# Layer 1's last chunks in another order of tiles, and layer 2's block products in rows of 14

## The chip, the cores and the metric

The kernel runs on one core of a Trainium2 chip. The metric is the device time of one execution in microseconds (us). Three runs of the kernel before gave 894.57, 895.60 and 896.61 us.

The engines are named as the profile names them: PE is TensorE (PEld its weight loads), DVE is VectorE, ACT is ScalarE, POOL is GpSimd and SP is SyncE, which here does nothing but issue transfers. Each engine takes its instructions in program order; PE, DVE, ACT and POOL run beside each other and wait for each other through semaphores.

## The reference

Windowed attention feeds a two-layer feed-forward pair. The attention comes first (4 batches, 8 heads, 576 positions, a window of 128); its output, 2304 tokens of 512 numbers, goes through two layers of the same form with different activations:

```python
def _moe_ref(x, w_in, w_out):
    h = x @ w_in                       # 2304x512 by 512x2048
    g = np.maximum(0.01 * h, h)
    return g @ w_out                   # 2304x2048 by 2048x512

def _moe2_ref(x, w_in, w_out):
    h = x @ w_in
    g = h * (1.0 / (1.0 + np.exp(-1.702 * h)))
    return g @ w_out
```

## The kernel before

The whole kernel is one hand-written order: `tick` advances a step counter, and `after(d, fn)` puts an instruction `d` steps later in the streams. Whatever is emitted earlier stands earlier in the queue of its engine. Every matrix operand is kept as a pair, a rounded part and a remainder (`hi` and `lo`), so each product is three passes (hi by hi, hi by lo, lo by hi).

**Layer 1.** The tokens lie in five tiles, t0 to t4, of 384, 512, 512, 512 and 384 columns; the 2048 hidden features lie in eight chunks of 256. `rounds` lists the pairs (chunk, tile). A round is two groups of `mm1` (L517, 12 matmuls each) and, one round later, four groups of `mm2` (L541, 6 matmuls each), whose result is added into `y` by DVE (L551). Chunk weights sit in two pairs of tiles, wA and wB, so the weights of chunk c+2 go where those of chunk c were; `conv_w` builds them on ACT, DVE and POOL from 64-bit words.

**Layer 2.** The 2304 tokens form six blocks of 384, taken as three pairs. `unit_ops(i, p)` multiplies pair p by the input weights of chunk i with seven block products (a Strassen-like scheme), each one `product` call of 6 matmuls with 384 columns (L623). Five of the seven accumulate into the same PSUM bank, `X` (tag S), one goes to `Y` (tag O), two into `Q` (tag pt). Between them ACT copies `X` aside (`snap`, L644, into `sn`), DVE adds `Y` or `Q` to a copy (`finish`, L649), ACT applies the activation (`gate`, L635, into `u`), and `split` makes hi (ACT, L532) and lo (POOL, L143) of the result, `g` or `gm`. Four gates make the hidden values of one pair. They are the stationary operand of the six output groups `out2` of that pair (L691, 6 matmuls with 512 columns), two PSUM banks of tag mm; DVE (ACT for chunk 0) adds each group into `y` (L703, L701).

Units run as (chunk 0, pair 0), (0, 1), (1, 0), (1, 1) and so on to chunk 7, then pair 2 with chunks 0 to 7. In the 13 places of a unit the seven products stand at 0, 2, 3, 5, 7, 9 and 11; the other six places, `None` in the list, hold the six output groups of the unit before (in the first unit, the last six `mm2` groups of layer 1). The products use the tokens through 14 derived blocks: `build_x(p, pace)` makes seven of them for a pair with seven ACT conversions (L588, 128x768) and eleven DVE operations (L143, 128x768, `x<-y` and `y<-y`), spread over 11 times `pace` steps. Pair 0's blocks are begun ten groups before the first product, pair 1's seven steps after it. Block weights are reloaded from DRAM by SP after their last use (`load_in`, L609); the output weights of chunks 1 to 7 are built during layer 2 (`conv_out`) from `raw` words that `load_w` fetches.

Of the kernel before, what the change touches and what calls it, by code (L numbers as in the profile page):

```python
# [22 lines left out]
CB = 2  # L23
# [10 lines left out]
def attention_mlp_kernel(  # L34
# [144 lines left out]
    def conv_w(n, p):  # L179
# [6 lines left out]
        else:  # L186
            af, ops = to_f32(n, p, 4)
        hi, lo = wt[n][:, 2 * p], wt[n][:, 2 * p + 1]
        run(ops + [
            (10 if early else 7, lambda: nc.scalar.activation(hi, af, AF.Copy)),  # L190
# [442 lines left out]
    def gate(h, key):  # L633
        u = sb([128, 512], F32, "u", 2)[:, 0:TT]
        nc.scalar.activation(u, h, AF.Gelu_apprx_sigmoid)  # L635
        after(1, lambda: split(u, key, True))

    def unit_ops(i, p):
# [84 lines left out]
    rounds += [(0, c, t) for c in range(2, NCH) for t in range(NTT)]  # L723
# [13 lines left out]

    last1 = {c: j for j, (_, c, _) in enumerate(rounds)}
# [19 lines left out]
    def layer1():  # L758
# [4 lines left out]
        while pos2[0] < NR - 4 or q1 or q2 or todo or pending[0]:  # L763
# [24 lines left out]
    def layer2():  # L788
# [17 lines left out]
        units = [(c, p) for c in range(NCH) for p in range(2)] + [  # L806
            (NCH + c, 2) for c in range(NCH)]
        prev = [run_group] * len(groups)
        for k, (i, p) in enumerate(units):
            more = i + 1 < NCH  # L810
            for t, fn in enumerate(unit_ops(i, p)):
                if more and (p, t) in ((0, 6), (1, 4)):
                    load_w(NF + CB * (i + 1) + p, 1)
                if more and (p, t) == (1, 1):
                    conv_out(NF + CB * (i + 1))
                if 0 < i < NCH and (p, t) == (0, 1):
                    conv_out(NF + CB * i + 1)
# [164 lines left out]
```

## Time and profile before

| | us |
|---|---|
| runs (median of 3) | 895.60 |
| profiled execution, its own time | 896.78 |
| its span, first to last instruction | 894.8 |
| PE busy | 869.0 |
| DVE busy | 592.0 |
| ACT busy | 422.5 |
| POOL busy | 400.1 |

The 2 us between the profiled execution and its span lie outside all instructions. A row of a timeline gives the start in us from the span's start, the duration, the engine, the line with its operation, out<-in, the shape and the number of merged instructions; in brackets stands how long the engine sat idle before it and what released it. Matmuls overlap, so the pace of PE is read from the start of one group to the start of the next, not from their durations.

### The profile page before, as it was taken

The page shows a single profiled execution, that of the slowest core. Times are in us where ns is not written, and L with a number is a line of the kernel's source. Part 1 is how long each engine was busy: PE and PEld are TensorE (multiplying, and loading weights), DVE is VectorE, ACT ScalarE, POOL GpSimd, SP SyncE. Part 2 cuts the span into 40 slices and gives each one's busy share as a digit, 9 for nine tenths or more (in the row PEclk, how much of TensorE's full clock was granted, in tenths as well). Part 3 has the DMA queues.
Part 4 walks back from the last instruction along what each step waited for, and adds up shares of the span by engine and source line. Part 5 has one row for each costly group of instructions (what it writes and reads, how often), then busy time and mean ns, then how long its engine had stood idle before and what let it go on. Part 6 is the DMA issues. An engine that isn't in the chain of part 4 may idle for free.

```text
span 894.8 us, 15722 instructions
## 1 busy us (share of the span) xinstructions
PE 869.0 (97%) x5722; PEld 762.4 (85%) x5722; DVE 592.0 (66%) x1213; ACT 422.5 (47%) x1025; POOL 400.1 (45%) x441
## 2 busy tenths in 40 slices
PE   7789999999999999999999989999999999999997
PEld 4678888899898988888898878888898889889896
DVE  5889765368799998898943773555555557423433
ACT  4888885454334433543333466343434435442331
POOL 5787544345466757575542133333333233232221
PEclk6899999999999999999999999999999999999999
DMA  9764330242243353524250133453354345956562
GB/s 218 172 168 118 99 92 5 92 132 80 71 140 146 115 174 132 177 82 172 100 188 1 48 104 96 153 153 95 107 153 132 93 129 153 293 174 204 164 188 71
DMA packets 85533, 116.05 MB, mean 130 GB/s; under 512 B 40912, under 2 KB 51152, under 8 KB 84432
## 3 DMA queue, kind: packets, MB, share of 16 engines
q1 hardware_dynamic: 82064, 113.83, 42.2%
q10 hardware_dynamic: 3392, 1.21, 0.5%
q8 instruction: 46, 0.75, 0.3%
q14 instruction: 31, 0.25, 0.1%
HBM read 87.23 MB, written 27.79 MB: 129 GB/s over the span
## 4 chain that ended last, share of the span: by engine, by line
PE 82%; DVE 6%; POOL 3%; DMA 3%; issue 2%; ACT 2%; SPq 0%; POOLq 0%; DVEq 0%; ACTq 0%
PE mm L691 22%; PE S L623 11%; PE mm L541 10%; PE O L541 8%; PE pt L517 8%; PE S L517 8%; PE pt L623 5%; PE O L623 3%; PE mm L517 2%; PE O L477 2%; PE pt L442 2%; PE S L393 2%; POOL ca L175 1%; DMA y<-v 1%; DVE x L143 1%
## 5 line engine op out<-in xcount | busy, mean ns | idle before, releaser
L143 POOL TENSOR_TENSOR g<-u,g 128x384 fp32r<-128x384 f32 (+1 forms) x128 | 155.6, 1221 | 244.0 <-ACT g L532 168.3
L703 DVE TENSOR_TENSOR y<-y,mm 128x512 f32<-128x512 f32 x126 | 86.5, 686 | 119.0 <-PE mm L691 118.8
L691 PE MATMUL mm<-wB,g 128*128 128x512 f32 x432 | 118.8, 397 | 0.6 <-POOL g L143 0.6
L691 PE MATMUL mm<-wB,gm 128*128 128x512 f32 x432 | 116.7, 393 | 0.0
L175 POOL TENSOR_TENSOR ca<-ca,cb 128x512 f32<-128x512 f32 x59 | 81.8, 1387 | 69.0 <-DVE cb L173 64.1
L143 POOL TENSOR_TENSOR gm<-u,gm 128x384 fp32r<-128x384 f32 x48 | 48.7, 1024 | 128.9 <-ACT gm L532 80.1
L691 PEld LDWEIGHTS mm<-wB,g 128*128 128x128 f32 x432 | 80.8, 189 | 13.6 <-POOL g L143 1.0
L691 PEld LDWEIGHTS mm<-wB,gm 128*128 128x128 f32 x432 | 80.1, 188 | 12.9
L635 ACT ACTIVATE u<-sn 128x384 f32<-128x384 f32 x72 | 37.8, 525 | 97.0 <-DVE sn L649 61.2
L623 PE MATMUL S<-x,wA 128*128 128x384 f32 x384 | 78.0, 337 | 2.3 <-ACT x L588 1.8
L623 PEld LDWEIGHTS S<-x,wA 128*128 128x128 f32 x384 | 68.3, 188 | 6.8 <-ACT x L588 2.1
L532 ACT ACTIVATE g<-u 128x384 fp32r<-128x384 f32 (+1 forms) x128 | 70.6, 560 | 2.5 <-PE O L541 0.6
L551 DVE TENSOR_TENSOR y<-y,mm 128x512 f32<-128x512 f32 (+1 forms) x74 | 46.2, 624 | 37.1 <-PE mm L541 37.0
L541 PE MATMUL mm<-g,wA 128*128 128x512 f32 (+1 forms) x264 | 62.9, 372 | 3.3 <-POOL g L143 2.5
L541 PE MATMUL mm<-g,wB 128*128 128x512 f32 (+1 forms) x264 | 62.3, 371 | 0.0
L523 ACT ACTIVATE u<-S 128x512 f32<-128x512 f32 (+1 forms) x34 | 18.8, 553 | 85.6 <-PE S L517 85.6
L623 PE MATMUL pt<-x,wA 128*128 128x384 f32 x288 | 57.9, 335 | 0.0
L644 ACT ACTIVATE sn<-S 128x384 f32<-128x384 f32 x72 | 34.9, 485 | 46.4 <-PE S L623 44.5
L541 PEld LDWEIGHTS mm<-g,wA 128*128 128x128 f32 x264 | 47.6, 188 | 10.2 <-POOL g L143 3.2
L165 DVE TENSOR_SCALAR ca<-ca 128x512 f32<-128x512 f32 x62 | 30.5, 492 | 38.8 <-ACT ca L164 38.7
L623 PEld LDWEIGHTS pt<-x,wA 128*128 128x128 f32 x288 | 51.6, 188 | 4.4
L436 POOL TENSOR_SCALAR st<-st,sm 128x192 f32<-128x192 f32 (+2 forms) x100 | 43.3, 453 | 25.6 <-PE pt L442 8.0
(127 smaller groups left out, 1797.2 us busy)
## 6 DMA issues: line engine op xcount, KB each, us to landing
wA<-w7d SPq DMA_DIRECT2D x112, 256.0 KB, 3.1
w7d<-c SPq DMA_DIRECT2D x8, 1792.0 KB, 7.1
wB<-wod SPq DMA_DIRECT2D x36, 256.0 KB, 5.1
raw<-w1i SPq DMA_DIRECT2D x16, 512.0 KB, 3.5
raw<-w1o SPq DMA_DIRECT2D x16, 512.0 KB, 3.6
raw<-w2o SPq DMA_DIRECT2D x16, 512.0 KB, 4.5
raw<-w2i SPq DMA_DIRECT2D x16, 512.0 KB, 3.5
wod<-wB SPq DMA_DIRECT2D x28, 256.0 KB, 3.5
```

Of the source, the lines that this page charges most:

```text
L143: e.tensor_tensor(out=out, in0=in0, in1=in1, op=ALU.subtract)
L175: lambda: nc.gpsimd.tensor_tensor(out=af, in0=af, in1=bf, op=ALU.add),
L436: nc.gpsimd.tensor_scalar(w, w, sm[s][:, 3, m:m + 1], 1.0, op0=ALU.mult, op1=ALU.mult)
L517: nc.tensor.matmul(out=h, lhsT=w[:, a, k * 128:(k + 1) * 128], rhs=xt[t][:, b2, k], start=(m == 0), stop=(m == len(ops) - 1),)
L532: nc.scalar.activation(g[:, 0], u, AF.Copy)
L541: nc.tensor.matmul(out=y, lhsT=wt[c * CB + f][:, 2 + a, e * 128:(e + 1) * 128], rhs=gt[r, f][:, b2, :], start=(m == 0), stop=(m == len(ops ...
L551: nc.vector.tensor_tensor(out=acc, in0=acc, in1=y, op=ALU.add)
L623: nc.tensor.matmul(out=out, lhsT=w[:, 256 * a + 128 * k:256 * a + 128 * k + 128], rhs=x[:, b2, k], start=(start and m == 0), stop=(stop an ...
L635: nc.scalar.activation(u, h, AF.Gelu_apprx_sigmoid)
L644: nc.scalar.activation(st[name], st["X"], AF.Copy)
L691: nc.tensor.matmul(out=y, lhsT=gt[i, p, f, t][:, b2, e * 128:(e + 1) * 128], rhs=out_slot(i, f, a), start=(m == 0), stop=(m == len(ops) - 1),)
L703: nc.vector.tensor_tensor(out=acc, in0=acc, in1=yv, op=ALU.add)
```

## The change

There are two parts. In layer 1, `rounds` takes the last two chunks in another order: chunks 6 and 7 with tiles 0 and 1, then chunks 6 and 7 with tiles 2, 3 and 4. `layer2` then begins its own code when chunk 7 is through with tile 1 (the loop of `layer1` ends there), and pair 0's blocks are built from that point at a pace of 2 steps, 28 groups before the first product; the first weight loads wait until chunk 6 is through with all tiles. In layer 2, the chunks 1 to 6 no longer alternate: the fourteen products of pairs 0 and 1 run in a row, then the twelve output groups of both pairs. Chunk 7 and the units of pair 2 keep one unit at a time, with products and output groups in runs of up to four and of two. Beside this the activation is written over the copy `sn` in three gates of four, in place of a tile of its own, and pair 1's blocks lie in another order in memory.

```diff
-            (10 if early else 7, lambda: nc.scalar.activation(hi, af, AF.Copy)),
+            (10 if early else 7, split_hi),
...
+        xb[1] = [xb[1][n] for n in (0, 1, 4, 3, 5, 2, 6)]
...
-    def gate(h, key):
-        u = sb([128, 512], F32, "u", 2)[:, 0:TT]
+    def gate(h, key, u=None):
+        u = sb([128, 512], F32, "u", 2)[:, 0:TT] if u is None else u
...
-                after(1, lambda: gate(h, (i, p) + key))
+                after(1, lambda: gate(h, (i, p) + key, h))
...
-    rounds += [(0, c, t) for c in range(2, NCH) for t in range(NTT)]
+    rounds += [(0, c, t) for c in range(2, NCH - 2) for t in range(NTT)]
+    rounds += [(0, c, t) for ts in ((0, 1), (2, 3, 4)) for c in (NCH - 2, NCH - 1) for t in ts]
...
-        while pos2[0] < NR - 4 or q1 or q2 or todo or pending[0]:
+        while pos2[0] < first or q1 or q2 or todo or pending[0]:
...
+        build_x(0, 2)
+        loaded = False
         while len(groups) > 6:
             run_group()
             tick()
-            if begun is None and pos2[0] >= NR - 4:
-                begun = step[0]
-                build_x(0, 1.6)
-        assert begun is not None
-        after(max(1, begun + 16 - step[0]), lambda: build_x(1, 1.3))
+            if not loaded and pos2[0] >= last1[NCH - 2]:
+                loaded = True
+                for n in USE:
+                    load_in(0, n)
+        assert loaded
+        after(len(groups) - 4 + 5, lambda: build_x(1, 1.3))
...
+        for i in range(1, NCH - 1):
+            n0 = NF + CB * (i + 1)
+            lead = [None] * (len(prev) if i == 1 else 0)
+            w = [unit_ops(i, p) for p in range(2)]
+            ops = lead + [w[p][n] for p, n in (
+                (0, 0), (1, 0), (0, 5), (0, 4), (1, 4), (1, 5), (0, 3), (1, 3), (0, 1), (0, 6),
+                (1, 6), (1, 1), (0, 2), (1, 2))]
+            tail = [fn for t in (1, 0) for p in range(2) for fn in outs(i, p, t)]
+            last = i == NCH - 2
+            m = len(ops)
+            at = {m - 10: [raw_out(n0)], m - 6: [raw_out(n0 + 1)], m: [make_out(n0)],
+                  m + 5: [make_out(n0 + 1)]}
...
+            play(ops + (tail[:6] if last else tail), at)
...
+        for i, p in [(NCH - 1, 0), (NCH - 1, 1)] + [(NCH + c, 2) for c in range(NCH)]:
+            w = unit_ops(i, p)
+            play([w[0], w[5], w[1], w[4], None, None, w[3], None, None, w[6], w[2], None, None], {})
...
-                after(1, lambda: build_x(2, 1.8))
+                after(1, lambda: build_x(2, 1.6))
```

PE in the middle of layer 2, at the start of the products of one chunk, before. L623 are block products, L691 output groups; S, O and pt are the banks X, Y and Q.

```order
L623 MATMUL S<-x,wA 128x384 x6
L691 MATMUL mm<-wB,g 128x512 x6
L623 MATMUL O<-x,wA 128x384 x6
L623 MATMUL S<-x,wA 128x384 x6
L691 MATMUL mm<-wB,g 128x512 x6
L623 MATMUL pt<-x,wA 128x384 x6
L691 MATMUL mm<-wB,g 128x512 x6
L623 MATMUL S<-x,wA 128x384 x6
L691 MATMUL mm<-wB,g 128x512 x3
L691 MATMUL mm<-wB,gm 128x512 x3
```

The same engine and place after the change (the product is L629 there); the last row is the first half of the first of twelve output groups.

```order
L629 MATMUL S<-x,wA 128x384 x12
L629 MATMUL pt<-x,wA 128x384 x6
L629 MATMUL S<-x,wA 128x384 x12
L629 MATMUL pt<-x,wA 128x384 x6
L629 MATMUL S<-xe,wA 128x384 x6
L629 MATMUL S<-x,wA 128x384 x6
L629 MATMUL O<-x,wA 128x384 x6
L629 MATMUL S<-xe,wA 128x384 x6
L629 MATMUL S<-x,wA 128x384 x6
L629 MATMUL O<-x,wA 128x384 x6
L629 MATMUL pt<-x,wA 128x384 x12
L691 MATMUL mm<-wB,gm 128x512 x3
```

What was one output group after every one or two products has become 84 matmuls of 384 columns and then 72 of 512.

ACT in the same stretch of layer 2 before: copies (L644), activations (L635), hi parts (L532) and pieces of `conv_out` (L164, L225).

```order
L635 ACTIVATE u<-sn 128x384
L532 ACTIVATE g<-u 128x384
L644 ACTIVATE sn<-S 128x384
L164 ACTIVATE ca<-raw 128x512
L635 ACTIVATE u<-sn 128x384
L644 ACTIVATE sn<-S 128x384
L532 ACTIVATE g<-u 128x384
L225 ACTIVATE wB<-ca 128x512
L644 ACTIVATE sn<-S 128x384
L635 ACTIVATE u<-sn 128x384
L635 ACTIVATE u<-S 128x384
L532 ACTIVATE g<-u 128x384 x2
```

ACT in one chunk after the change: copies are L650, activations L641, hi parts L537.

```order
L650 ACTIVATE sn<-S 128x384 x6
L641 ACTIVATE sn<-sn 128x384 x2
L537 ACTIVATE g<-sn 128x384
L641 ACTIVATE sn<-sn 128x384
L641 ACTIVATE u<-S 128x384
L537 ACTIVATE g<-sn 128x384 x2
L537 ACTIVATE gm<-u 128x384
L641 ACTIVATE u<-S 128x384
L537 ACTIVATE gm<-u 128x384
L641 ACTIVATE sn<-sn 128x384
L537 ACTIVATE gm<-sn 128x384
L641 ACTIVATE sn<-sn 128x384
```

All six copies now come first and the eight gates of both pairs follow each other without other work between; the first hi part stands behind two activations.

ACT at the start of layer 2 before: L588 are the conversions of `build_x`, the table load belongs to the first activation.

```order
L588 ACTIVATE x<-y 128x768
L644 ACTIVATE sn<-S 128x384
L588 ACTIVATE x<-y 128x768
L588 ACTIVATE xe<-y 128x768
L635 ACT_TABLE_LOAD
L635 ACTIVATE u<-sn 128x384
L644 ACTIVATE sn<-S 128x384
L588 ACTIVATE x<-y 128x768
L532 ACTIVATE g<-u 128x384
L588 ACTIVATE x<-y 128x768 x2
L644 ACTIVATE sn<-S 128x384
```

The same place after the change (L594 are the conversions there).

```order
L650 ACTIVATE sn<-S 128x384
L641 ACT_TABLE_LOAD
L641 ACTIVATE sn<-sn 128x384
L650 ACTIVATE sn<-S 128x384
L537 ACTIVATE g<-sn 128x384
L594 ACTIVATE x<-y 128x768 x2
L650 ACTIVATE sn<-S 128x384
L594 ACTIVATE x<-y 128x768
```

The conversions of pair 0 are gone from here (they stand among the last rounds of layer 1); those of pair 1 stand where they stood.

## Rows read from the trace of the kernel before

**Rows 1.** Page, part 1: busy us, share of the span, instructions.

```profile
PE 869.0 (97%) x5722; PEld 762.4 (85%) x5722; DVE 592.0 (66%) x1213; ACT 422.5 (47%) x1025; POOL 400.1 (45%) x441
```

**Rows 2.** Busy by stretch: PE, PEld, DVE, ACT, POOL, granted clock, DMA share, GB/s.

```profile
522.80:527.50 4.70, 4.32 (x12) 3.49 (x13) 4.67 (x8) 2.29 (x4) 0.00 (x0) 0.64 0.31 95
...
560.00:700.00 140.00, 140.00 (x699) 125.79 (x698) 78.02 (x135) 57.34 (x117) 47.13 (x46) 1.00 0.43 133
```

**Rows 3.** Timeline of layer 2's steady part, PE: products and output groups in turn.

```profile
604.80 1.55 PE L691 MATMUL mm<-wB,gm 128*128 128x512 f32 x6
606.19 1.20 PE L623 MATMUL pt<-x,wA 128*128 128x384 f32 x6
607.23 1.55 PE L691 MATMUL mm<-wB,gm 128*128 128x512 f32 x6
```

**Rows 4.** Timeline of the kernel's end, DVE: addition of one of six output groups.

```profile
888.81 0.69 DVE L703 TENSOR_TENSOR y<-y,mm 128x512 f32<-128x512 f32 x1 [0.67 <-PE mm L691]
```

**Rows 5.** Timeline of layer 1, PE: three groups of 512 columns after one of 384.

```profile
313.15 2.92 PE L517 MATMUL S<-x,wA 128*128 128x512 f32 x12
315.91 2.88 PE L517 MATMUL pt<-x,wA 128*128 128x512 f32 x12
318.63 0.69 PE L541 MATMUL mm<-g,wA 128*128 128x384 f32 x3
```

**Rows 6.** Timeline of one gate of layer 2: DVE add, product, activation, hi parts, lo parts.

```profile
610.39 0.56 DVE L649 TENSOR_TENSOR sn<-sn,pt 128x384 f32<-128x384 f32 x1
...
611.06 1.21 PE L623 MATMUL S<-xe,wA 128*128 128x384 f32 x6
612.36 0.49 ACT L635 ACTIVATE u<-S 128x384 f32<-128x384 f32 x1 [0.85 <-PE S L623]
612.75 0.93 ACT L532 ACTIVATE g<-u 128x384 fp32r<-128x384 f32 x2
613.34 2.00 POOL L143 TENSOR_TENSOR g<-u,g 128x384 fp32r<-128x384 f32 x2 [4.28 <-ACT g L532]
```

**Rows 7.** Groups by form, 540 to 740 us, POOL: count, busy us, mean ns, idle before.

```profile
L143 POOL TENSOR_TENSOR g<-u,g 128x384 fp32r<-128x384 f32 x28 | 28.3, 1019 | 68.0 <-ACT g L532 38.1 <-issue 28.0 <-PE S L623 1.9
```

**Rows 8.** Timeline of POOL at the start of layer 2.

```profile
510.46 1.53 POOL L143 TENSOR_TENSOR g<-u,g 128x384 fp32r<-128x384 f32 x1 [9.28 <-ACT g L532]
```

**Rows 9.** Timeline at the start of layer 2, PE, ACT and DVE: pair 1's blocks come late.

```profile
514.65 0.95 DVE L143 TENSOR_TENSOR x<-y,x 128x768 fp32r<-128x768 f32 x1
...
515.98 1.66 DVE L143 TENSOR_TENSOR x<-y,x 128x768 fp32r<-128x768 f32 x1
...
518.02 1.29 DVE L143 TENSOR_TENSOR y<-y 128x768 f32<-128x768 f32 x1
518.55 1.42 PE L691 MATMUL mm<-wB,g 128*128 128x512 f32 x5 [0.57 <-POOL g L143]
519.35 0.85 ACT L588 ACTIVATE x<-y 128x768 fp32r<-128x768 f32 x1 [0.63 <-DVE y L143]
521.91 1.57 ACT L588 ACTIVATE x<-y 128x768 fp32r<-128x768 f32 x2
522.80 0.62 PE L623 MATMUL S<-x,wA 128*128 128x384 f32 x2 [1.77 <-ACT x L588]
523.80 1.41 PE L623 MATMUL S<-x,wA 128*128 128x384 f32 x4 [0.37 <-DVE x L143]
```

**Rows 10.** Timeline of the same stretch, PE alone: its first and last groups, and one wait.

```profile
501.49 1.23 PE L623 MATMUL S<-x,wA 128*128 128x384 f32 x6
...
512.22 1.34 PE L623 MATMUL S<-xe,wA 128*128 128x384 f32 x6 [0.47 <-ACT sn L644]
...
533.90 0.86 PE L691 MATMUL mm<-wB,g 128*128 128x512 f32 x3
```

**Rows 11.** Timeline of layer 1: a round of chunk 6 and the last weights of chunk 7.

```profile
434.18 1.07 PE L517 MATMUL S<-x,wA 128*128 128x512 f32 x4
...
441.12 0.68 DVE L143 TENSOR_TENSOR wB<-ca,wB 128x512 fp32r<-128x512 f32 x1
```

More of the change, by code (lines that the diff above doesn't have):

```diff
@@ L188, in conv_w, with split_hi @@
         hi, lo = wt[n][:, 2 * p], wt[n][:, 2 * p + 1]
+        def split_hi():
+            assert slot_free(n, p)
+            nc.scalar.activation(hi, af, AF.Copy)
         run(ops + [
-            (10 if early else 7, lambda: nc.scalar.activation(hi, af, AF.Copy)),
+            (10 if early else 7, split_hi),
             (12 if early else 8, lambda: (
@@ L736, in attention_mlp_kernel @@
     groups.reverse()
+    first = rounds.index((0, NCH - 1, 1))
     last1 = {c: j for j, (_, c, _) in enumerate(rounds)}
@@ L800, in layer2, with outs, play @@
             tick()
-            if begun is None and pos2[0] >= NR - 4:
-                begun = step[0]
-                build_x(0, 1.6)
-        assert begun is not None
-        after(max(1, begun + 16 - step[0]), lambda: build_x(1, 1.3))
-        units = [(c, p) for c in range(NCH) for p in range(2)] + [
-            (NCH + c, 2) for c in range(NCH)]
-        prev = [run_group] * len(groups)
[L809 to L817, printed above, removed]
+            if not loaded and pos2[0] >= last1[NCH - 2]:
[4 more added lines that the diff above has]
+        after(len(groups) - 4 + 5, lambda: build_x(1, 1.3))
+        prev = [run_group] * len(groups)
+        def outs(i, p, t):
+            return [lambda e=e: out2(i, p, t, e) for e in range(3)]
+        def play(ops, at):
+            for t, fn in enumerate(ops):
+                for g in at.get(t, ()):
+                    g()
                 if fn is not None:
@@ L822, in layer2, with raw_out, make_out @@
                 tick()
-            if p and NCH - 1 <= i < 2 * NCH - 1:
+        def raw_out(n):
+            return lambda: load_w(n, 1)
+        def make_out(n):
+            return lambda: conv_out(n)
+        n0 = NF + CB
+        for p in range(2):
+            w = unit_ops(0, p)
+            play([w[0], None, w[1], w[4], None, w[5], None, w[3], None, w[6], None, w[2], None],
+                 {4: [raw_out(n0 + 1)], 1: [make_out(n0)]} if p else {6: [raw_out(n0)]})
+            if not p:
+                load_out(0)
+            prev = outs(0, p, 1) + outs(0, p, 0)
+        for i in range(1, NCH - 1):
[10 more added lines that the diff above has]
+                  m + 5: [make_out(n0 + 1)]}
+            if i == 1:
+                at[1] = [make_out(NF + CB + 1)]
+            play(ops + (tail[:6] if last else tail), at)
+            if last:
+                prev = tail[6:]
+        for i, p in [(NCH - 1, 0), (NCH - 1, 1)] + [(NCH + c, 2) for c in range(NCH)]:
+            w = unit_ops(i, p)
+            play([w[0], w[5], w[1], w[4], None, None, w[3], None, None, w[6], w[2], None, None], {})
+            if p and i < 2 * NCH - 1:
                 load_out(i + 1)
-            if k == 0:
-                load_out(0)
             if (i, p) == (NCH - 1, 0):
-                after(1, lambda: build_x(2, 1.8))
-            prev = [lambda t=t, e=e, i=i, p=p: out2(i, p, t, e) for t in (1, 0) for e in range(3)]
+                after(1, lambda: build_x(2, 1.6))
+            prev = outs(i, p, 1) + outs(i, p, 0)
         for _ in range(4):
```

29 lines of the change are left out of this document (10 added, 19 removed).

## The prediction, made before the changed kernel had run

> **What bounds the kernel now.** I read the page first, then busy time by stretch, then PE's timeline where it falls below full. PE is busy for 869.0 of 894.8 us, the next engine for 592.0 [rows 1], and from 560 to 700 us PE is busy all the time at the full granted clock of 1.00, that is 2.4 GHz [rows 2]. So inside layer 2 a change can help only by making PE's own pace better, and it can hurt by putting a wait where there is none.
>
> The pace: an output group of six matmuls that stands between products takes 606.19 - 604.80 = 1.39 us, a product 607.23 - 606.19 = 1.04 us [rows 3]. At the kernel's end, where six output groups follow each other, DVE adds one every 0.69 + 0.67 = 1.36 us and waits for PE each time [rows 4]. Layer 1 says the same: twelve 512-column matmuls right after 384-column ones take 315.91 - 313.15 = 2.76 us, the next twelve 318.63 - 315.91 = 2.72, again 1.36 for six [rows 5]. A run of equal width is thus a little faster, and its start costs 0.04.
>
> The second place is the start of layer 2. From 501.49 to 533.90 us [rows 10] PE does 17 groups of 384 columns and 6 of 512, which take 17 x 1.04 + 6 x 1.39 = 26.0 us undisturbed; it took 32.4. These 6.4 us are waits: before 512.22 [rows 10], before 518.55 for a lo part from POOL, before 522.80 for an ACT conversion (1.77 idle) and before 523.80 for its DVE remainder [rows 9]. After them the granted clock was 0.64 on average for 4.7 us, between the levels of 2.4 and 1.2 GHz [rows 2]: about 0.36 x 4.7 = 1.7 of the 6.4.
>
> **Part 1: runs of 14 and 12 in chunks 1 to 6.** Twelve output groups save 12 x 0.03 = 0.36 us per chunk. Against that stand two changes of width, 0.04 from 384 to 512 and an estimated 0.03 back: 0.29 net, times six chunks **-1.7 us**. The bounds are 0, if the interleaved pace stays, and -2.2 if the changes cost nothing. The last ten units get runs of four and two: 30 pairs of output groups, each 2.76 in place of 2.78, against 30 returns to 384 columns at up to 0.03; I take zero, between -0.6 and +0.3.
>
> *The new wait it can bring.* Twelve output groups need eight gates that all come late in the fourteen products. Say the first product starts at 0. Its twelve followers come every 1.04 us. Pair 1's third copy follows product 8, which starts at 7.29; an ACT instruction on a product starts 612.36 - 611.06 = 1.30 after that product does and a copy takes about the 0.49 of that row: 8.59 to 9.08. DVE's add (0.56) ends at about 9.65, the activation starts right behind it at 9.69, and behind it in ACT's queue stands the first hi part; two such instructions of 0.52 take 0.93 together, so the pace is 0.41 [rows 6]: 10.10. ACT then issues two activations and three hi parts, the third ending at 10.10 + 5 x 0.41 + 0.52 = 12.67. POOL begins the first lo part at 10.69, the second when its hi part is there at 11.92, and the next two behind it at 0.98 each (two took 2.00 [rows 6]), so the fourth ends at 14.90. That fourth, of pair 0's last X, is what the second matmul of the first output group reads. PE gets there at 14 x 1.04 + 0.03 + 0.23 = 14.8. I price the wait at 0.15 us with what a late weight load adds: 6 x 0.15 = **+0.9 us**. The ends are 0 and, if POOL's 1.02 [rows 7] becomes the 1.53 it took beside DVE's block building [rows 8], 0.15 + 4 x 0.5 = 2.15 per chunk, 12.9 in all. I stay at the low end because DVE's adds in that phase are the same L649 adds beside which POOL ran at 1.02.
>
> *Cover of the rest.* With two mm banks, a group in a run must be added before the next but one begins; DVE has 0.67 us free per group [rows 4]. Two `conv_out` put up to 12 more DVE operations into the 12 x 1.36 = 16.3 us of the run; were each as long as an addition, 24 x 0.69 = 16.6 would just fill it, and the last of them falls behind the run. I take nothing, and 0.3 per chunk as the far end. X, Y and Q have two banks each, one per pair, and each copy has at least one other product before its bank is written again: nothing. On SP the block weights are reloaded after pair 1's products and are needed a whole run of twelve later; the raw loads stand ten places ahead of their first use: nothing. Writing the activation over `sn` frees ACT from waiting for POOL to give back `u`; that wait was off the path: nothing. The assertion and the new places of pair 1's blocks add no instruction: nothing.
>
> **Part 2: layer 1's order and the early blocks.** Chunk 7 with tile 0 takes the place of the round that began at 434.18; the last of its weights were written at 441.12 + 0.68 = 441.80 [rows 11]. Those are output weights, needed after that round's products, four `mm2` groups and another round's products, 4.2 + 5.4 + 5.4 = 15 us later, at about 449: 7 us to spare. The seven first block loads (1.8 MB) are issued when chunk 6 is done, and the first product is a round of `mm1`, four `mm2` groups, a narrow round of `mm1` and two more groups away, 5.4 + 5.4 + 4.2 + 2.7 = 17.7 us; at the 133 GB/s of the steady part [rows 2] they take 13.8: nothing.
>
> Pair 0's seven conversions and eleven DVE operations leave the stretch from 501.49 on; in layer 1 they lie beside 28 groups. That removes the wait before 512.22 (0.64 us) and, since the gates of the first unit no longer queue behind them, the one before 518.55 (0.8).
>
> It does not remove the longest. Pair 1's blocks begin at the same step as before, and the path is DVE, then ACT in order: a conversion waited for a DVE difference, started at 519.35, and the conversion that PE waited for ended at 521.91 + 0.85 = 522.75, 3.40 us later, behind a hi part, a copy, a `conv_out` step and an addition [rows 9]. Counted from the first product, PE reaches that product at 13 x 1.04 + 3 x 1.39 = 17.7 undisturbed. DVE must first add the `mm2` group that ends at 12.2 (estimated 0.6, and 0.2 to be released), do a block remainder (0.95 to 1.66 [rows 9]), a gate's add (0.56 [rows 6]) and the difference (0.95 to 1.29 [rows 9]): the conversion starts at 15.4 to 16.3, not at the 519.35 - 501.49 = 17.9 of before, and 3.40 later it is 18.8 to 19.7. PE waits 1.1 to 2.0, then about 0.6 for the remainder, and a few tenths later in the unit: I take 2.6 us. So the loss of 6.4 becomes 2.6, **-3.8 us**, if the clock stays up. It fell before after 1.77 us of idle time that followed other waits; here the others are gone. If it falls again 1.7 comes back. The ends are -0.5 and -5.9.
>
> **Sum.** -1.7 + 0.9 - 3.8 = -4.6 us against the profiled execution's 896.8 (span 894.8 and 2 outside it), 892.2. That execution is 1.2 above the median of 895.6, so the same change gives **891.0** for a median.
>
> **Rivals.**
> - *Both covers hold.* The first output group never waits and the blocks of pair 1 come 0.5 us late at most: -1.7 - 5.9 = -7.6, 888.0. For it speaks that my DVE times at the start of layer 2 are taken with POOL beside them; against it ACT's queue of 3.40, which is unchanged.
> - *The run is no faster.* If 1.36 belongs to the end of the kernel and to layer 1, where the operands come from elsewhere, runs in mid-layer keep 1.39: 0.9 - 3.8 = -2.9, 892.7. The Trainium skill, TensorE: Matmul & The Clock Gate, section "Wait — 56ns, not 53.3ns?", speaks for this one: it gives bf16 matmuls a start-to-start time of columns by 2.4 GHz plus about 2.5 ns, whatever came before, which would be 1.30 us for six of 512 and no gain from runs. The trace differs in size (1.36 and 1.39) and has two paces, so I follow the trace.
> - *The start of layer 2 stays as it is.* If ACT's queue alone sets when pair 1's blocks are ready, PE only waits there longer in one piece and the clock falls again: the gain is 0.5, and -1.7 + 0.9 - 0.5 = -1.3, 894.3. The change then does not do what its second part says.
> - *POOL is late in every chunk, slower than before.* All eight gates end together and POOL does them one by one before PE's first output group. At 1.53 us each the wait is 12.9 in all: -1.7 + 12.9 - 3.8 = +7.4, 903.0. It decides from 5.5 / 6 = 0.9 us per chunk, which is POOL at some 1.2 us instead of 1.02, or ACT 0.8 later than I laid out. Against it: POOL's 1.02 in 28 of 28 [rows 7].
>
> **How the numbers follow.** Forecast 0.50, own range 889 to 893; both covers 0.12; no faster run 0.13; start unchanged 0.13; POOL late 0.09; the remaining 0.03 are small waits that I have not seen, 0.01 on each side. A measurement of this kernel can tell about 0.2% from no change, 1.8 us: faster is below 893.8. Faster: 0.50 + 0.12 + 0.13 + 0.01 = 0.76; same: 0.13 + 0.01 = 0.14; slower: 0.09 + 0.01 = 0.10. The range leaves out POOL's case above and half of the best one below: 887.5 to 895.3.
>
> **What would show it.** Output groups 1.36 us apart inside a run of twelve and products 1.04 apart (part 1); a wait of 0 to 0.4 us for POOL before the second matmul of each run of twelve, from 0.9 on the last rival; no wait at pair 0's sixth product and none at the first output group; one wait for an ACT conversion at pair 1's fourth place of products, 1 to 2 us, and a granted clock of 1.00 behind it. I am wrong if any wait of over 0.5 us recurs in chunks 1 to 6, or if PE stops in layer 1 after 434 us.

## The result: 902.5 us, slower by 0.7%

Four runs of the changed kernel gave 901.37 to 903.50 us, median 902.48; four of the kernel before beside them 894.57 to 896.61, median 895.56. The ratio is 1.0073, 95% interval [1.0059, 1.0087]: slower, where 891.0 and "faster" were forecast. The profiled execution after took 903.47 us, 6.7 more than the one before (896.78).

### The profile page after: what moved, and what is told of

Read it like the earlier page. It is cut to its first block, busy times and chain, and to the rows that moved or that the text cites. A ratio compares the mean times of both kernels' runs of the same rounds, so it can differ in the third digit from the quotient of the medians.

```text
span 901.8 us, 15696 instructions
## 1 busy us (share of the span) xinstructions
PE 870.8 (97%) x5722; PEld 761.0 (84%) x5722; DVE 597.7 (66%) x1213; ACT 422.5 (47%) x1025; POOL 400.0 (44%) x441
## 4 chain that ended last, share of the span: by engine, by line
PE 79%; DVE 8%; DMA 4%; POOL 3%; issue 3%; ACT 2%; SPq 0%; POOLq 0%; DVEq 0%; ACTq 0%
PE mm L691 21%; PE S L629 10%; PE mm L546 9%; PE pt L522 8%; PE O L546 7%; PE S L522 7%; PE pt L629 5%; PE O L629 3%; PE mm L522 2%; PE O L482 2%; PE S L398 2%; PE pt L447 2%; DVE ca L169 1%; DMA raw<-w1i 1%; POOL ca L175 1%
## 5 line engine op out<-in xcount | busy, mean ns | idle before, releaser
L143 POOL TENSOR_TENSOR g<-u,g 128x512 fp32r<-128x512 f32 (+1 forms) x86 | 112.8, 1315 | 129.9 <-ACT g L537 106.9
L691 PE MATMUL mm<-wB,gm 128*128 128x512 f32 x432 | 118.4, 395 | 0.2
L691 PE MATMUL mm<-wB,g 128*128 128x512 f32 x432 | 118.5, 395 | 0.0
L143 POOL TENSOR_TENSOR g<-sn,g 128x384 fp32r<-128x384 f32 x42 | 43.6, 1044 | 131.6 <-ACT g L537 100.8
L691 PEld LDWEIGHTS mm<-wB,gm 128*128 128x128 f32 x432 | 79.3, 188 | 21.2 <-POOL gm L143 2.4
L691 PEld LDWEIGHTS mm<-wB,g 128*128 128x128 f32 x432 | 81.5, 190 | 17.0 <-POOL g L143 0.4
L629 PE MATMUL S<-x,wA 128*128 128x384 f32 x384 | 76.5, 338 | 2.3 <-ACT x L594 1.8
L655 DVE TENSOR_TENSOR sn<-sn,pt 128x384 f32<-128x384 f32 x48 | 26.6, 554 | 77.2 <-ACT sn L650 52.8
L650 ACT ACTIVATE sn<-S 128x384 f32<-128x384 f32 x72 | 35.3, 491 | 85.7 <-PE S L629 85.6
L629 PEld LDWEIGHTS S<-x,wA 128*128 128x128 f32 x384 | 68.1, 189 | 5.0 <-ACT x L594 2.1
L143 POOL TENSOR_TENSOR gm<-sn,gm 128x384 fp32r<-128x384 f32 x30 | 31.8, 1069 | 65.4 <-ACT gm L537 51.0
L528 ACT ACTIVATE u<-S 128x512 f32<-128x512 f32 (+1 forms) x34 | 18.8, 553 | 89.2 <-PE S L522 89.2
L629 PE MATMUL pt<-x,wA 128*128 128x384 f32 x288 | 57.0, 334 | 0.5 <-DVE x L143 0.5
L167 DVE TENSOR_SCALAR ca<-ca 128x512 uint32<-128x512 uint32 x62 | 56.0, 904 | 0.5
L169 DVE SCALAR_TENSOR_TENSOR ca<-raw,ca 128x512 uint32<-128x512 uint32 x62 | 55.1, 888 | 0.6
```

What stands on the lines that cost most here:

```text
L143: e.tensor_tensor(out=out, in0=in0, in1=in1, op=ALU.subtract)
L167: lambda: nc.vector.tensor_scalar(a, a, 0x07FFFFFF, 3, op0=ALU.bitwise_and, op1=ALU.logical_shift_left),
L169: lambda: nc.vector.scalar_tensor_tensor(out=a, in0=hi32, scalar=0xC0000000, in1=a, op0=ALU.bitwise_and, op1=ALU.bitwise_or),
L629: nc.tensor.matmul(out=out, lhsT=w[:, 256 * a + 128 * k:256 * a + 128 * k + 128], rhs=x[:, b2, k], start=(start and m == 0), stop=(stop an ...
L650: nc.scalar.activation(st[name], st["X"], AF.Copy)
L691: nc.tensor.matmul(out=y, lhsT=gt[i, p, f, t][:, b2, e * 128:(e + 1) * 128], rhs=out_slot(i, f, a), start=(m == 0), stop=(m == len(ops) - 1),)
```

## The profile after

The page's first part and three stretches of the changed kernel (us, then busy us of PE, PEld, DVE, ACT, POOL, the granted clock, DMA share, GB/s):

```profile
PE 870.8 (97%) x5722; PEld 761.0 (84%) x5722; DVE 597.7 (66%) x1213; ACT 422.5 (47%) x1025; POOL 400.0 (44%) x441
```

```profile
428.80:432.20 3.40, 3.40 (x11) 3.40 (x12) 3.40 (x7) 0.89 (x2) 0.70 (x1) 0.51 0.43 161
526.50:531.35 4.85, 4.41 (x13) 3.56 (x14) 4.77 (x8) 2.44 (x5) 0.00 (x0) 0.65 0.32 94
560.00:700.00 140.00, 139.86 (x689) 122.46 (x688) 84.16 (x135) 56.70 (x121) 52.91 (x49) 1.00 0.39 124
```

The same work is done (the instruction counts are those of [rows 1]); PE is busy 1.8 us longer and idle 5.2 us longer. The second stretch, the start of layer 2, has the granted clock of [rows 2] again, 0.65 against 0.64. The first, in layer 1, is new: a clock of 0.51, practically the lower level of 1.2 GHz, for 3.4 us. The third, mid-layer 2, is at full clock but no longer without gaps.

**Layer 1.** PE and ACT of the changed kernel around that stretch, then PE and ACT of the kernel before at the same place:

```profile
424.47 2.25 PE L522 MATMUL S<-x,wB 128*128 128x384 f32 x12
428.80 3.87 PE L522 MATMUL pt<-x,wB 128*128 128x384 f32 x12 [2.09 <-ACT wB L192]
432.51 1.55 PE L546 MATMUL mm<-g,wA 128*128 128x512 f32 x6
...
428.12 0.63 ACT L192 ACTIVATE wB<-ca 128x512 fp32r<-128x512 f32 x1 [3.29 <-POOL ca L175]
```

```profile
423.26 2.92 PE L517 MATMUL S<-x,wA 128*128 128x512 f32 x12
...
426.96 0.63 ACT L190 ACTIVATE wB<-ca 128x512 fp32r<-128x512 f32 x1 [3.34 <-POOL ca L175]
```

Before, the round that begins at 423.26 is chunk 6 with tile 2; its weights lie in wA. After, chunk 7 with tile 0 stands there and needs wB. Its second feature half waits 2.09 us for a weight that ACT finishes at 428.12 + 0.63 = 428.75, and its twelve matmuls then take 432.51 - 428.80 = 3.71 us where twelve of 384 columns take 2 x 1.04 = 2.08. It could have begun at 424.47 + 2.08 = 426.55: 2.25 us of waiting and 1.63 of slow matmuls, 3.9 together. The weight is no later than it was: in the kernel before it was ready at 426.96 + 0.63 = 427.59, and everything else in this stretch is 1.2 us earlier there too. It is needed a round too soon.

**The start of layer 2.** PE, ACT and one step of DVE of the changed kernel (pair 1's first unit, to be compared with [rows 9]; the first product starts at 506.58):

```profile
506.58 1.23 PE L629 MATMUL S<-x,wA 128*128 128x384 f32 x6
...
526.56 0.62 PE L629 MATMUL S<-x,wA 128*128 128x384 f32 x2 [1.75 <-ACT x L594]
527.56 1.53 PE L629 MATMUL S<-x,wA 128*128 128x384 f32 x4 [0.37 <-DVE x L143]
...
523.11 0.85 ACT L594 ACTIVATE x<-y 128x768 fp32r<-128x768 f32 x1 [1.10 <-DVE y L143]
523.86 0.51 ACT L537 ACTIVATE gm<-sn 128x384 fp32r<-128x384 f32 x1
524.27 0.47 ACT L650 ACTIVATE sn<-S 128x384 f32<-128x384 f32 x1
524.64 0.66 ACT L164 ACTIVATE ca<-raw 128x512 f32<-128x512 f32 x1
525.20 0.58 ACT L701 ACTIVATE y<-mm 128x512 f32<-128x512 f32 x1
525.67 1.57 ACT L594 ACTIVATE x<-y 128x768 fp32r<-128x768 f32 x2
...
521.37 1.70 DVE L143 TENSOR_TENSOR y<-y 128x768 f32<-128x768 f32 x1
```

The waits before 512.22 and 518.55 of [rows 9, 10] are down to 0.3 us together, all of it at the first output group. The third stands as it was: ACT begins the first conversion at 523.11, when DVE's difference has ended (521.37 + 1.70 = 523.07), runs four other instructions and reaches the conversion that PE waits for at 525.67. From the first product to the output group that starts at 537.66 (the one at 533.90 in [rows 10]) it is 31.08 us, 26.0 of it work by the prediction's reckoning: 5.1 lost, against 6.4.

**A chunk of layer 2.** PE, PEld, POOL and DVE of the changed kernel at the head of a run of twelve output groups, and PE at the head of the next run:

```profile
595.83 1.16 PE L691 MATMUL mm<-wB,gm 128*128 128x512 f32 x3
596.83 0.86 PE L691 MATMUL mm<-wB,g 128*128 128x512 f32 x3
...
605.25 0.84 PE L691 MATMUL mm<-wB,gm 128*128 128x512 f32 x3
...
606.61 0.84 PE L691 MATMUL mm<-wB,gm 128*128 128x512 f32 x3
...
627.47 1.16 PE L691 MATMUL mm<-wB,gm 128*128 128x512 f32 x3
...
596.26 0.30 PEld L691 LDWEIGHTS mm<-wB,gm 128*128 128x128 f32 x2 [0.41 <-POOL gm L143]
...
595.20 1.99 POOL L143 TENSOR_TENSOR gm<-u,gm 128x384 fp32r<-128x384 f32 x2
597.14 2.18 POOL L143 TENSOR_TENSOR gm<-sn,gm 128x384 fp32r<-128x384 f32 x2
...
598.33 1.28 DVE L167 TENSOR_SCALAR ca<-ca 128x512 uint32<-128x512 uint32 x1
599.53 0.68 DVE L703 TENSOR_TENSOR y<-y,mm 128x512 f32<-128x512 f32 x1
```

Output groups are 606.61 - 605.25 = 1.36 us apart, as [rows 4, 5] had it. But a chunk takes 627.47 - 595.83 = 31.64 us; the interleaved order takes 31.28. Three small pieces recur in every chunk, read as matmul start to matmul start less the pace: 0.31 at the head of the run (the second weight load waits 0.41 for POOL's fourth remainder), 0.17 ahead of the fourth group (it needs the bank of the second, whose addition starts at 599.53 only, behind a `conv_out` step of 1.28), and 0.11 later, where both `conv_out` share DVE with the additions. They make 0.6 per chunk.

**Pair 2's first unit.** POOL, DVE and PE of the changed kernel:

```profile
762.60 1.01 POOL L143 TENSOR_TENSOR g<-sn,g 128x384 fp32r<-128x384 f32 x1 [1.24 <-PE mm L691]
...
762.70 1.72 DVE L143 TENSOR_TENSOR x<-y,x 128x768 fp32r<-128x768 f32 x1
...
763.49 0.51 PE L629 MATMUL pt<-x,wA 128*128 128x384 f32 x2
...
764.48 0.97 PE L629 MATMUL pt<-x,wA 128*128 128x384 f32 x4 [0.47 <-DVE x L143]
```

The product that stood at place 5 of a unit now stands at place 1, and the remainder of its block is not there: 0.75 us.

The sum, in the two traces: +3.9 in layer 1, -1.3 at the start of layer 2, +2.0 in the chunks taken together (0.36 in a full one), +0.75 in pair 2 and +0.45 after the last matmul, 5.8 in all. The spans, 901.8 and 894.8, differ by 7.0. The other 1.2 is there before the orders part (424.47 against 423.26). Up to that point both kernels do the same work, and the nine experiments reach it between 1.9 us earlier and 1.4 us later than the kernel before does, so this part is scatter between executions. Why the last 0.45 is there is open: runs 2, 3 and 5 have it too, runs 1, 4 and 6 to 9 do not.

## Experiments

Each run was timed against the kernel before on the same chip, so the ratios can be compared from row to row; "lost at the start" is the time from the first product to the output group of [rows 10] less 26.0, as above.

| run | median us | ratio [95%] | lost at the start | per chunk |
|---|---|---|---|---|
| before | 895.6 to 896.7 | 1 | 6.4 | 31.28 |
| after | 902.48 | 1.0073 [1.0059, 1.0087] | 5.1 | 31.64 |
| 1 layer 1 only | 898.36 | 1.0023 [1.0008, 1.0037] | 5.1 | as before |
| 2 layer 2 only | 898.01 | 1.0022 [1.0008, 1.0035] | 5.5 | as after |
| 3 chunk 7 later | 898.22 | 1.0017 [1.0005, 1.0029] | 5.1 | as after |
| 4 two remainders on DVE | 897.82 | 1.0012 [1.0002, 1.0022] | 5.1 | 31.12 |
| 5 run 3 + block order | 897.88 | 1.0027 [1.0016, 1.0037] | 5.5 | as after |
| 6 run 5 + chunks and pair 2 mended | 893.18 | 0.9973 [0.9963, 0.9983] | 5.5 | 30.94 |
| 7 runs 1 + 3 + block order | 895.32 | 0.9994 [0.9984, 1.0004] | 5.5 | 31.28 |
| 8 run 6 + `conv_out` later | 888.90 | 0.9921 [0.9908, 0.9935] | 2.0 | as run 6 |
| 9 run 8 + blocks earlier | 887.98 | 0.9911 [0.9895, 0.9926] | 1.2 | as run 6 |

My theory after the two traces: three separate losses (weights of chunk 7, POOL and DVE in the chunks, pair 2's first unit) beside a start of layer 2 that gained too little. The rival: the runs of 14 and 12 carry most of the loss, and the wait in layer 1 only moves time that is lost later anyway.

**Run 1: layer 1's part alone.** Layer 2 is played in units as before.

```diff
-        for i in range(1, NCH - 1):
...
-            w = [unit_ops(i, p) for p in range(2)]
...
+        for k, (i, p) in enumerate(units):
+            w = unit_ops(i, p)
...
+            play([w[0], None, w[1], w[4], None, w[5], None, w[3], None, w[6], None, w[2], None], at)
```

> The order of layer 1 and the early blocks as in the changed kernel, layer 2 interleaved unit by unit as in the kernel before. Theory (the loss is a sum of small waits in separate places: 3.9 us for chunk 7's input weights near 428 us, 2.0 us in chunks 1 to 6, 0.75 at pair 2's second product, against 1.5 gained at the start of layer 2): this part alone gives +3.9 - 1.5 = +2.4 us, about 898, with 31.28 us per chunk of two pairs. Rival (POOL late in every run of twelve is the whole loss): nothing is lost here, and the time is 1.5 to 4 us below the kernel before, 892 to 894.

898.36. The wait for wB is there in full (PE stands 2.09 us before 428.14, the same releaser), the start loses 5.1, the chunks take 31.28. Layer 1's part alone is a loss, by 2.6 us in the trace from the point where the orders part.

**Run 2: layer 2's part alone.**

```diff
-    rounds += [(0, c, t) for c in range(2, NCH - 2) for t in range(NTT)]
-    rounds += [(0, c, t) for ts in ((0, 1), (2, 3, 4)) for c in (NCH - 2, NCH - 1) for t in ts]
+    rounds += [(0, c, t) for c in range(2, NCH) for t in range(NTT)]
...
-        build_x(0, 2)
...
+            if begun is None and pos2[0] >= NR - 4:
+                begun = step[0]
+                build_x(0, 1.6)
```

> Layer 1 and the start of the blocks as in the kernel before, layer 2 as in the changed kernel. Theory of separate waits: +2.0 in chunks 1 to 6 (31.6 us per chunk in place of 31.3) and +0.75 at pair 2's second product, so +2.8, about 898.3, and no wait near 428 us. Rival (the whole loss is in layer 2): +7 or more, 902 and above.

898.01. No wait in layer 1; the three pieces per chunk and the one in pair 2 are there, at the same size. The two parts lose about 2 us each and neither needs the other for it. By the medians, 2.1 and 1.7 us, the parts add up to 4.7 of the 6.9 by which after's median was slower, once the gain at the start (1.3 and 0.9), which both contain, is counted once. That leaves 2.2 us, and each of the three ratios is known to about 1.3 us only. The traces place it: from the point where the orders part to the end, the kernel before takes 471.6 us (its span less the 423.26 at which that round starts), run 1 474.2, run 2 474.0 and after 477.3. That is 2.6 and 2.5, or 5.9 with the start's gain counted once, against 5.7. So the parts do add up.

Run 2 has pair 0's conversions where the kernel before has them, and yet the wait before 512.22 [rows 10] is gone. ACT's table load, before and in run 2:

```profile
506.98 1.28 ACT L635 ACT_TABLE_LOAD   x1 [2.27 <-DVE sn L649]
```

```profile
502.83 1.28 ACT L641 ACT_TABLE_LOAD   x1
```

Before, the load waited 2.27 us until DVE's addition was done, and the first activation stood behind it. In run 2, where the activation is written over `sn`, it ran while ACT had nothing else to do. It does so in after and run 1 too.

**Run 3: chunk 6's tile 2 ahead of chunk 7's first rounds.**

```diff
-    rounds += [(0, c, t) for ts in ((0, 1), (2, 3, 4)) for c in (NCH - 2, NCH - 1) for t in ts]
+    rounds += [(0, NCH - 2, t) for t in (0, 1, 2)] + [(0, NCH - 1, t) for t in (0, 1)]
+    rounds += [(0, NCH - 2, t) for t in (3, 4)] + [(0, NCH - 1, t) for t in (2, 3, 4)]
```

> The changed kernel with chunk 6's tile 2 moved ahead of chunk 7's first two tiles, which gives the weights of chunk 7 one more round of about 11 us. Theory: the wait of 2.25 us near 428 us goes and with it the half clock behind it, 3.9 us in all: about 898.6. Rival (the wait there comes from the DVE backlog of the weight building and moves with it): the time stays at 902 to 903 and a wait of over 1 us stands before another product of chunk 7.

898.22. PE of this run, first half of each of two rounds: chunk 6's tile 2 again from 423.58, chunk 7's tile 0 from 434.50.

```profile
423.58 2.92 PE L522 MATMUL S<-x,wA 128*128 128x512 f32 x12
...
434.50 2.27 PE L522 MATMUL S<-x,wB 128*128 128x384 f32 x12
```

No bracket, no stretched group: moving one round 11 us later takes the whole 3.9 us away, and it does not come back later: from that round to the first product it is 78.3 us, against 82.1 in after and 78.2 before. The cause is shown, and the rival, that the wait moves on, is out.

**Run 4: two of the eight remainders of a chunk on DVE.**

```diff
-        sub(nc.gpsimd, g[:, 1], u, g[:, 0].bitcast(F32))
+        dve = more and 1 <= key[0] < NCH - 1 and key[1:] in ((1, 1, 1), (0, 0, 0))
+        sub(nc.vector if dve else nc.gpsimd, g[:, 1], u, g[:, 0].bitcast(F32))
```

> The changed kernel, but in chunks 1 to 6 the remainders of two of eight gates (pair 1's third copy and pair 0's first copy) are made by DVE instead of POOL, so that pair 0's last X reaches POOL second instead of fourth. Theory (POOL's queue sets the wait at the head of each run of twelve): the 0.3 us there goes, and with POOL through two us earlier most of the 0.15 at the third output group, 6 x 0.45 = 2.7 us: about 899.8. Rival (ACT's queue or DVE sets it): no change within 0.5 us, 902 to 903.

897.82. PE, POOL and DVE of this run at the head of a run of twelve:

```profile
595.99 0.86 PE L692 MATMUL mm<-wB,gm 128*128 128x512 f32 x3
596.68 0.85 PE L692 MATMUL mm<-wB,g 128*128 128x512 f32 x3
...
597.46 1.02 POOL L143 TENSOR_TENSOR gm<-sn,gm 128x384 fp32r<-128x384 f32 x1 [0.25 <-ACT gm L537]
...
598.18 0.58 DVE L167 TENSOR_SCALAR ca<-ca 128x512 uint32<-128x512 uint32 x1
```

The first three matmuls take the 0.69 of the pace in place of the 1.00 of after: POOL did set the head of the run. With it went the 0.17 ahead of the fourth group: DVE's `conv_out` step now ends at 598.18 + 0.58 = 598.76, 0.28 after the POOL remainder that was under way when it began (597.46 + 1.02 = 598.48). In after it ended 0.29 behind POOL's as well (597.14 + 2.18 = 599.32 and 598.33 + 1.28 = 599.61), but it had begun as that remainder did (599.32 - 1.01 = 598.31) and so stood for all of it. The 0.11 stays. That is 0.5 per chunk, 3.0 in all. The median fell by more than was expected, 4.7 for 2.7, and the traces place only the 3.0.

**Run 5: one conversion of pair 1 ahead of its neighbour.**

```diff
-            (6, diff(b22, b22, b11)), (6, hi(3, b12)), (7, hi(2, b22)), (7, lo(2, b22, V)),
+            (6, diff(b22, b22, b11)),
+            *(((6, hi(2, b22)), (7, hi(3, b12))) if p == 1 else ((6, hi(3, b12)), (7, hi(2, b22)))),
+            (7, lo(2, b22, V)),
```

> The third run's kernel (the round of chunk 6 with tile 2 ahead of chunk 7's first rounds), and one more exchange: among pair 1's conversions the one of the first block that a product waits for is issued one step ahead of its neighbour, so that it stands one 1.25 us of ACT work earlier in ACT's queue. Theory, ACT's order sets the last long wait at the start of layer 2: the wait there shrinks from 2.2 us in one piece to about 1.0, PE's idle time no longer brings the half clock, and of the 3.9 us lost there 1.3 to 1.5 stay. That is 2.4 to 2.9 us less than the third run's 898.2: 895.5, within 0.5 us of the kernel before. Rival, DVE's difference or the remainder sets it, or the clock falls all the same: 898 (896.8 if the wait gets shorter and the half clock stays).

897.88 where 895.5 was expected, so nothing: the theory of ACT's queue fell. PE, ACT and DVE of this run, and its granted clock from the wait on:

```profile
519.71 0.62 PE L631 MATMUL S<-x,wA 128*128 128x384 f32 x2 [1.32 <-ACT sn L652]
521.59 1.65 PE L631 MATMUL S<-x,wA 128*128 128x384 f32 x4 [1.26 <-DVE x L143]
...
518.02 0.84 ACT L594 ACTIVATE x<-y 128x768 fp32r<-128x768 f32 x1 [2.44 <-DVE y L143]
...
519.19 0.47 ACT L652 ACTIVATE sn<-S 128x384 f32<-128x384 f32 x1
519.56 0.66 ACT L164 ACTIVATE ca<-raw 128x512 f32<-128x512 f32 x1
...
520.25 0.43 DVE L165 TENSOR_SCALAR ca<-ca 128x512 f32<-128x512 f32 x1 [2.25 <-ACT ca L164]
520.59 0.95 DVE L143 TENSOR_TENSOR x<-y,x 128x768 fp32r<-128x768 f32 x1
```

```profile
519.70:525.18 5.48, 4.21 (x13) 3.44 (x14) 4.90 (x9) 3.95 (x7) 0.66 (x1) 0.69 0.25 74
```

The conversion is ready at 518.86, before PE needs it. PE now waits first for the copy (behind the conversion in ACT's queue, which itself stood 2.44 us for DVE), then for the remainder, and that could have run at 518.9: DVE was idle. But ahead of it in DVE's queue stands the second step of `conv_out` (L165), which waited 2.25 us for ACT's first step. The long wait became two of 1.3, and the clock fell again.

**Run 6: run 5 with the chunks and pair 2 mended.** Run 4's edit, and:

```diff
-                  m + 5: [make_out(n0 + 1)]}
+                  m + (5 if last else 6): [make_out(n0 + 1)]}
...
+            if i == NCH:
+                play([w[0], None, w[1], w[4], None, w[5], None, w[3], None, w[6], None, w[2], None], {})
+            else:
+                play([w[0], w[5], w[1], w[4], None, None, w[3], None, None, w[6], w[2], None, None], {})
-            play([w[0], w[5], w[1], w[4], None, None, w[3], None, None, w[6], w[2], None, None], {})
```

> The kernel of the run above (block exchange), with every further cause mended: in chunks 1 to 6 two of the eight remainders on DVE in place of POOL (as in the fourth run), pair 2's first unit with its second product at its old place, and the second piece of output weights one output group later. Theory, the causes are separate and add up: from 895.5, 3.0 less for the remainders (the fourth run against after: 4.7 less; of these 1.4 were not in the waits of the chunks and I do not count on them), 0.75 less for pair 2's first unit, 0.3 to 0.6 less for the output weights: 891.2, ratio 0.995. Rival, runs of 14 and 12 only shift waits: the time gained at the head of the runs comes back as DVE late in the additions: 893 to 895.

893.18, 4.7 under run 5 where 4.3 was expected; the absolute figure was missed because run 5 had gained nothing. In chunks 1 to 6 and in pair 2 no wait of PE above 0.1 us is left: with the second `conv_out` one group later the 0.11 of run 4 is gone too, 30.94 per chunk for 31.12.

**Run 7: layer 2 interleaved, on the same layer 1 and start.** Run 1's `units` loop with the edits of runs 3 and 5:

```diff
+    rounds += [(0, NCH - 2, t) for t in (0, 1, 2)] + [(0, NCH - 1, t) for t in (0, 1)]
...
+            *(((6, hi(2, b22)), (7, hi(3, b12))) if p == 1 else ((6, hi(3, b12)), (7, hi(2, b22)))),
...
+        for k, (i, p) in enumerate(units):
```

> The first run's kernel (layer 1's order and the early blocks; layer 2 alternates products and output groups as before), with chunk 6's tile 2 moved ahead and the block exchange: no wait for weights in layer 1, the start of layer 2 as in the run with the exchange. Theory: 898.4 - 3.9 at layer 1's round - 2.4 at the start of layer 2 = 892.1, ratio 0.996. If runs of 14 and 12 with all waits mended are worth their pace (0.29 us per chunk, 1.7 in all), this one is slower than the kernel above by 0.9 to 1.7 us; rival, the runs are worth nothing: the two agree within 0.5 us.

895.32, 2.1 over run 6 (0.9 to 1.7 expected; 892.1 was missed because the exchange had gained nothing). PE at the head of two successive runs of output groups in run 6, and at the same product of two successive chunks in run 7:

```profile
590.24 0.86 PE L694 MATMUL mm<-wB,gm 128*128 128x512 f32 x3
...
621.18 0.86 PE L694 MATMUL mm<-wB,gm 128*128 128x512 f32 x3
```

```profile
598.74 1.21 PE L631 MATMUL S<-x,wA 128*128 128x384 f32 x6
...
630.02 1.21 PE L631 MATMUL S<-x,wA 128*128 128x384 f32 x6
```

30.94 against 31.28: without its waits the run order is worth 0.34 us per chunk, 2.0 in all. The prediction's first term, 0.29 and 1.7, was right; the changed kernel had hidden it under 31.64 - 30.94 = 0.70 per chunk, of which the three pieces are 0.6.

**Run 8: run 6, with `conv_out` of pair 1's first unit six places later.**

```diff
-                 {4: [raw_out(n0 + 1)], 1: [make_out(n0)]} if p else {6: [raw_out(n0)]})
+                 {4: [raw_out(n0 + 1)], 7: [make_out(n0)]} if p else {6: [raw_out(n0)]})
```

> The mended kernel (893.2) with one more move: during pair 1's first unit the first step of the output weights (which makes DVE stand for ACT, with the block remainder that PE waits for behind it) begins six places later. Theory, DVE's queue set the second half of the wait: the remainder runs as soon as its conversion is there, the 1.26 us wait between the product's second and third matmul goes, the wait for the copy (1.3) stays, and of the 5.7 us lost at the start of layer 2 about 4.4 stay if the clock falls all the same (891.9), about 2.8 if it does not (890.3). Rival, the remainder is late by itself (DVE's other block work): no change, 893.2.

888.90. PE of this run and its granted clock behind the wait:

```profile
521.62 1.33 PE L632 MATMUL S<-x,wA 128*128 128x384 f32 x6 [1.32 <-ACT sn L653]
```

```profile
521.60:526.60 5.00, 4.97 (x24) 4.47 (x25) 4.29 (x6) 4.47 (x8) 1.62 (x2) 1.00 0.60 205
```

The wait for the copy is the same 1.32; the one for the remainder is gone, and with it the half clock: 2.0 lost in place of 5.5, less than the 2.8 of the better of the two cases expected. The place of an unrelated step was worth 3.5 us here by the trace (4.3 by the medians, 4.7 by the ratios).

**Run 9: run 8, pair 1's blocks one step earlier, the conversion behind the copy.**

```diff
-            *(((6, hi(2, b22)), (7, hi(3, b12))) if p == 1 else ((6, hi(3, b12)), (7, hi(2, b22)))),
+            *(((7, hi(2, b22)), (7, hi(3, b12))) if p == 1 else ((6, hi(3, b12)), (7, hi(2, b22)))),
...
-        after(len(groups) - 4 + 5, lambda: build_x(1, 1.3))
+        after(len(groups) - 4 + 4, lambda: build_x(1, 1.3))
```

> The kernel of the run above, with pair 1's blocks begun one step earlier and the conversion that PE waits for put behind the copy of the running sums in ACT's queue, not ahead of it. Theory, ACT's order and DVE's order together set the start: no wait there is longer than 0.7 us, the clock stays at its higher level, and of the 5.7 us lost 1.0 to 2.0 stay: 889.0 to 890.0, ratio 0.993. Rival, DVE's block work as a whole is the bound (it is busy without a gap from 508 to 518): the wait for the conversion stays over 1 us and the clock falls again: 891 to 892.

887.98, the best of all: 0.9911 of the kernel before. PE of this run:

```profile
519.07 1.43 PE L694 MATMUL mm<-wB,g 128*128 128x512 f32 x5 [0.84 <-POOL g L143]
520.34 1.23 PE L632 MATMUL O<-x,wA 128*128 128x384 f32 x6
521.41 1.20 PE L632 MATMUL S<-x,wA 128*128 128x384 f32 x6
```

The product that had waited in every kernel so far starts 1.07 after its predecessor. What is late next is a lo part of pair 0, at the first output group: 0.84, the wait that [rows 9] shows as 0.57. So the expectation of no wait above 0.7 us was missed, and the time is 1 us below the range it gave. From run 8 it is a gain of 0.8 us by the trace; the 0.9 of the medians lies within the intervals of the two ratios. What the placements of runs 8 and 9 would give the kernel before, with its own order, was not run.

## Why the prediction was wrong

The forecast was -4.6 us, and the spans differ by +7.0. Of the 11.6 between them 3.9 are layer 1's order, 2.8 the chunks (+2.0 for -0.8), 2.5 the start of layer 2, 0.75 pair 2, and 1.65 the two pieces ahead of the change and behind the last matmul.

- **The failed step: layer 1's order at nothing.** The prediction put chunk 7 with tile 0 in the place of the round at 434.18 [rows 11] and found 7 us to spare. That row is chunk 6 with tile 3. The changed order puts (7, 0) right behind (6, 1), so the place is that of (6, 2), at 423.26, 10.9 us earlier: one count of rounds, not done. And the weights to ask for were the input weights of the round's own products, needed at once, not the output weights at 441.80 that are needed 15 us later. It cost +3.9 (run 3), and turned a forecast that would have read 895 into 891. No rival and no end of the range held it.
- **The new wait at the head of a run**: right mechanism and place (POOL's fourth remainder, PE's second weight load), wrong size: 0.31 for 0.15 per chunk. The layout of ACT and POOL from [rows 6] held to about 0.1 us; the late weight load, which is priced in the 0.15, waited 0.41 itself.
- **"Cover of the rest: nothing"** for DVE in the run: the sum of DVE's work fitted, but not each addition. 0.17 + 0.11 per chunk, within the far end of 0.3. DVE's L167 took 1.28, not the 0.69 reckoned for each, because it ended 0.29 behind the POOL remainder at whose start it began.
- **The last rival, POOL late in every chunk at 1.53,** did not happen: POOL's remainders up to the one that PE waited for took 1.0 each. That its 903.0 lies near the 902.5 measured is luck.
- **Runs of equal width**: right. 1.36 apart, 0.34 per chunk once the waits are gone (runs 6 and 7) against 0.29. The rival "the run is no faster" is out. The Trainium skill (TensorE: Matmul & The Clock Gate, "Wait — 56ns, not 53.3ns?"), which the prediction weighed beside it, gives back-to-back matmuls of one width one start-to-start time. Here six of 512 columns take 1.36 or 1.39 us by what stands ahead of them, so for this kernel one time per width is not enough. (The third row of [rows 5] is of 384 columns, not of 512 as its heading has it; only its start is used.)
- **The start of layer 2**: -1.3 for -3.8. That the first two waits go was right, but for 0.3. For the first of them the reason given, pair 0's conversions, was not needed: run 2 lost that wait with the conversions in place, when the table load no longer waited for DVE. What differs there in run 2 is the activation over `sn`, which the prediction put at nothing; no run tests it alone. For the third wait, the conversion started 523.11 - 506.58 = 16.5 after the first product and ended at 19.9. The prediction said 15.4 to 16.3 and 18.8 to 19.7, but its own terms add up to 15.5 to 16.5; DVE's difference took 1.70 us where it had at most 1.29. So the wait was 1.75 + 0.37 where 1.1 to 2.0 + 0.6 stood. The mis-sized term was the clock: it fell as before, although "the others are gone", and the 1.7 named for that came back. The forecast with it is 4.3 lost against 5.1. The rival's reason, ACT's queue, is not the whole of it: with that queue reordered (run 5) DVE's order behind `conv_out` held PE for as long, and mending that (run 8) gave 3.5.
- **Pair 2's units at zero**: right for units in steady state, wrong for the first, where pair 2's blocks are just being built: 0.75, not seen.
- **The test that was set** named a stop in layer 1 "after 434 us" and a wait above 0.5 us in the chunks. PE stopped at 426.7 and waited 0.31, so neither sign showed, although the forecast was wrong: the first looked past the place.

What stays open: why the last 0.45 us of after come behind its last matmul, why run 4's median fell by 1.7 us more than its trace shows, and what sets the scatter of up to 3.3 us at 423 us.

## What to carry to other kernels

When a change permutes rounds, write out both orders and pair them by position before reading any "time to spare": the row that a round replaces is the one at its new index. A step that makes an engine wait for another (here `conv_out`: ACT, then DVE) is a barrier for everything behind it in that queue, so look for it just ahead of the work that PE waits for; moving it cost nothing and gave 3.5 us. A change that measures as a loss can hold a gain: here the two ideas, with six placements mended, run at 0.9911 of the kernel before. Of the 7.2 us that run 9 gains there from the first product to the last matmul, 2.0 are the run order (runs 6 and 7) and 5.2 the start of layer 2.

## What the runs showed of the hardware

Idle time of PE and the granted clock behind it: 0.84 us (run 9, 1.00 in the stretch below) and 1.32 us (run 8, 1.00) left the clock at 2.4 GHz; 1.32 and 1.26 us with two matmuls between them (run 5, 0.69 over 5.5 us), 1.75 and 0.37 (after, 0.65) and 2.09 in one piece (after, 0.51) were followed by the lower level. Run 9, the stretch behind its wait:

```profile
519.00:524.00 5.00, 4.93 (x24) 4.44 (x25) 4.41 (x6) 3.52 (x6) 0.99 (x2) 1.00 0.43 108
```

So the price of a wait of this kind is not its length alone: the second wait of run 5 was 1.26 us long and its removal gave 3.5.

How long a step of DVE takes beside POOL depends on which of the two began first. Take the 128x768 block operations of DVE (L143) from 420 us on, in all eleven traces. The 260 that began with no POOL remainder under way took 0.94 to 0.96 us. The other 103 began while one was under way, and 102 of them ended 0.81 to 0.91 us behind that remainder's end, whatever that made of their length: the one at 762.70 took 1.72 and ended at 764.42, 0.81 behind the remainder that ended at 762.60 + 1.01 = 763.61. The `conv_out` step L167 ended 0.28 to 0.29 us behind it in 48 of 48 cases between 540 and 760 us, and so took 1.28 in after and 0.58 in run 4.
